# Soft-capped attention with a soft-MoE layer: head pairs on 128 partitions, column-tiled matmuls, slot sums inside the attention, casting weight loads

## Chip, cores, metric

One core of one Trainium2 chip. The metric is the device time of one execution in microseconds (us). Times are medians of all executions of a kernel. An execution more than 1.5% above the fastest of its kernel counts as slow, and the ratios leave it out.

The engines by their short names: PE multiplies matrices (its weight loads are counted apart), ACT applies functions such as tanh and exp, DVE does vector arithmetic and copies, POOL here casts v and issues the casting loads, and DMA moves data between memory and chip. PSUM is the memory that PE writes into. P·V is the product of the exps with v.

## The reference, cut to what matters

```python
# q, k, v: (8 batches, 12 heads, 448 positions, 64); q, k about 0.1 in size; cap = 30
scores = (1 / sqrt(64)) * q @ k.T
scores = cap * tanh(scores / cap)
x = softmax(scores) @ v                    # -> x: (3584, 768)
logits = x @ phi                           # phi: (768, 32), 8 experts x 4 slots
slot_input = softmax(logits, axis=0).T @ x # (32, 768): over all 3584 positions
slot_out[e] = relu(slot_input[e] @ w1[e]) @ w2[e]   # w1 (8,768,1024), w2 (8,1024,768)
out = softmax(logits, axis=1) @ slot_out   # (3584, 768)
```

All inputs are fp32: q, k and v are 33 MB, w1 and w2 25.2 MB each, the output 11 MB. No expert can start before the last position is through the attention.

## The kernel before

One head at a time. A head's 448 keys are four tiles of 112 partitions, so one tanh and one exp of 112x1792 elements cover it.

```python
for b in range(B):
    for h in range(H):
        # loads of q, k, v; cast of v; transposes of q and k in fp32; copies
        sc = psA.tile([C, NC, 512], F32, tag="sc")          # C = 112, NC = 4, one buffer
        for c in range(NC):
            nc.tensor.matmul(sc[:, c, :S], kT[:, c, :], qTf, start=True, stop=True)
        th = attn.tile([C, NC, S], BF16, tag="th")
        nc.scalar.activation(th, sc[:, :, :S], ACT.Tanh, scale=qk_scale / cap)
        ex = attn.tile([C, NC, S], BF16, tag="ex")
        nc.scalar.activation(ex, th, ACT.Exp, scale=cap)
        ot = psB.tile([Dh + 1, 512], F32, tag="ot", bufs=1)
        for c in range(NC):
            nc.tensor.matmul(ot[:, :S], vaug[:, c, :], ex[:, c, :],
                             start=(c == 0), stop=(c == NC - 1))
        # copy, transposes back, reciprocal, product -> xbuf
# after all heads: transposes of xbuf, logits, exp, transposes, slot sums   (cut)
for e in range(E):
    # w1 matmuls with 4 output rows, relu, transposes                       (cut)
    for fh in range(NFT // 2):
        w2f = moeW.tile([P, 2, D], F32, tag="w2f", bufs=3)
        nc.sync.dma_start(out=w2f, in_=w2r[:, e, 2 * fh:2 * fh + 2, :])
        nc.vector.tensor_copy(w2b[:, 2 * fh:2 * fh + 2, :], w2f)
    # w2 matmuls, transposes                                                (cut)
for nt in range(NNT):                                        # 32 stores
    # two matmuls into op
    osb = moeY.tile([C, 2, HD], F32, tag="osb")              # three buffers
    nc.scalar.mul(osb, op[:, :, :HD], Winv[:, nt:nt + 1])
    nc.sync.dma_start(out=dstap, in_=osb.rearrange("p a b -> p (a b)"))
```

The softmax here doesn't subtract the row's maximum and nothing guards it: scores larger than these inputs give would overflow.

## Time and profile before

| stage | from, to (us) | length | what fills it |
|---|---|---|---|
| start | 0 to 13.5 | 13.5 | loads, casts, transposes up to the first tanh |
| attention | 13.5 to 346 | 332 | ACT, tanh and exp |
| logits, slot sums | 346 to 394 | 48 | PE and ACT in turns, DMA nearly idle |
| experts | 394 to 472 | 78 | the load of w2 |
| output | 472 to 521 | 49 | stores from three buffers |

The stretches below are those stages in the trace of the kernel before. The columns are the stretch, its length, the busy time (and number of instructions) of PE, PE's weight loads, DVE, ACT and POOL, then PE's clock, the DMA share and GB/s.

```profile
13.00:346.00 333.00, 301.13 (x1901) 185.36 (x1900) 278.23 (x877) 313.09 (x192) 0.00 (x0) 0.97 0.54 167
346.00:394.00 48.00, 43.06 (x474) 25.63 (x473) 9.57 (x45) 31.91 (x102) 0.00 (x0) 0.73 0.22 81
394.00:472.00 78.00, 66.47 (x342) 24.95 (x340) 38.08 (x141) 16.22 (x32) 0.00 (x0) 0.80 0.80 275
472.00:521.00 49.00, 24.70 (x64) 11.74 (x63) 0.00 (x0) 28.59 (x32) 0.00 (x0) 0.50 0.71 225
```

ACT is busy for 313 of 333 us in the attention. In the 48 us after it the DMA share is 0.22, and up to 382 us it is 0.01 or less: nothing is loaded while the logits are made, and the experts then wait for w2.

### The profile page before, as it was taken

The numbers are of one execution on the slowest core, as the hardware profiler recorded it, in microseconds if no ns is written. First come the engines' busy times: TensorE is split into PE (matmuls) and PEld (weight loads), VectorE is DVE, ScalarE is ACT, GpSimd is POOL, SyncE is SP. The second block draws the span as 40 slices with busy tenths as digits, with TensorE's granted clock in tenths as the row PEclk, the third lists the DMA queues.
The fourth block names the chain that finished last, engine by engine and source line by source line (L and its number), as shares of the span: only waits on it lengthen the run. The fifth ranks groups of instructions, "written<-read, shape, count | busy, mean of one in ns | idle before, by whom it ended". The sixth has DMA issues, their size and how long they took to land.

```text
span 521.0 us, 8045 instructions
## 1 busy us (share of the span) xinstructions
PE 439.2 (84%) x2790; PEld 250.2 (48%) x2790; DVE 329.1 (63%) x1069; ACT 391.1 (75%) x359; POOL 1.3 (0%) x8
## 2 busy tenths in 40 slices
PE   2999898889999989999989998879979997766552
PEld 1555465555555555555555555534564333223220
DVE  2588678888888888888888889840044545441000
ACT  0689589999999999999999998966962231115664
POOL 0000000000000000000000000000000000000000
PEclk9999679999999999999999999965969999555555
DMA  8669555474565554565554533200059798964776
GB/s 242 229 183 316 163 160 170 132 248 126 180 187 186 178 180 133 171 187 187 173 182 134 180 108 97 66 8 0 1 193 355 255 328 284 316 208 153 245 244 205
DMA packets 57016, 95.00 MB, mean 182 GB/s; under 512 B 6800, under 2 KB 39056, under 8 KB 56976
## 3 DMA queue, kind: packets, MB, share of 16 engines
q1 hardware_dynamic: 56976, 94.49, 56.6%
q8 instruction: 22, 0.36, 0.3%
q14 instruction: 18, 0.15, 0.1%
HBM read 83.46 MB, written 11.01 MB: 181 GB/s over the span
## 4 chain that ended last, share of the span: by engine, by line
ACT 54%; PE 24%; DMA 14%; DVE 5%; issue 1%; SPq 1%; ACTq 0%; DVEq 0%
ACT ex L130 26%; ACT th L127 24%; DMA out_dram<-osb 6%; PE hp L234 4%; DMA w2f<-in_moe_w_dram 4%; PE sop L258 3%; PE xtp L182 3%; PE lt L190 3%; PE sc L123 3%; DMA vraw<-in_v_dram 2%; PE ot L134 2%; ACT osb L308 2%; PE qTp L108 2%; DVE w2b L253 1%; PE kTp L115 1%
## 5 line engine op out<-in xcount | busy, mean ns | idle before, releaser
L127 ACT ACTIVATE th<-sc 112x1792 bf16<-112x1792 f32 x96 | 158.1, 1647 | 27.0 <-PE sc L123 27.0
L130 ACT ACTIVATE ex<-th 112x1792 bf16<-112x1792 bf16 x96 | 162.9, 1697 | 3.0
L123 PE MATMUL sc<-qT,kT 64*112 64x448 bf16 x384 | 106.9, 372 | 17.7 <-ACT th L127 16.2
L134 PE MATMUL ot<-ex,vaug 112*65 112x448 bf16 x384 | 93.5, 367 | 9.2 <-ACT ex L130 8.8
L137 DVE CAST ot_sb<-ot 65x448 bf16<-65x448 f32 x96 | 59.5, 619 | 22.1 <-PE ot L134 20.2
L108 PE MATMUL qTp<-ident,qraw 112*64 112x112 f32 x384 | 62.6, 274 | 11.4 <-DVE qT L111 5.8
L148 DVE TENSOR_SCALAR xbuf<-ott,rec 112x64 bf16<-112x64 bf16 x384 | 68.3, 235 | 0.1
L123 PEld LDWEIGHTS <-kT 64*112 64x112 bf16 x384 | 44.7, 128 | 43.0 <-issue 31.0
L111 DVE CAST qT<-qTp 64x448 bf16<-64x448 f32 x96 | 58.3, 607 | 7.7 <-PE qTp L108 6.6
L115 PE MATMUL kTp<-ident,kraw 112*64 112x112 f32 x384 | 58.2, 272 | 0.8 <-DVE kT L118 0.7
L118 DVE CAST kT<-kTp 64x448 bf16<-64x448 f32 x96 | 57.1, 595 | 2.7 <-PE kTp L115 2.5
L134 PEld LDWEIGHTS <-vaug 112*65 112x65 bf16 x384 | 43.3, 114 | 31.2 <-issue 16.2
L108 PEld LDWEIGHTS qTp<-ident,qraw 112*64 112x64 f32 x384 | 36.6, 116 | 34.4 <-issue 11.4
L115 PEld LDWEIGHTS kTp<-ident,kraw 112*64 112x64 f32 x384 | 40.2, 117 | 13.5 <-issue 3.3
L141 PEld LDWEIGHTS <-ot_sb 65*112 65x112 bf16 x384 | 28.1, 134 | 37.6 <-DVE vaug L100 16.8
L308 ACT ACTIVATE osb<-op,Winv 112x768 f32<-112x768 f32 x32 | 28.6, 900 | 18.6 <-DMA out_dram<-osb 15.3
L141 PE MATMUL ott<-ident_bf,ot_sb 65*112 65x65 bf16 x384 | 38.6, 226 | 2.6 <-DVE ot_sb L137 2.6
L258 PE MATMUL sop<-w2b,hTb 128*4 128x384 bf16 x128 | 36.5, 393 | 4.2 <-DVE w2b L253 3.9
L303 PE MATMUL op<-so,ET 32*112 32x384 bf16 x64 | 24.8, 499 | 17.3 <-ACT osb L308 16.4
L253 DVE CAST w2b<-w2f 128x1536 bf16<-128x1536 f32 x32 | 30.3, 952 | 9.3 <-DMA w2f<-in_moe_w_dram 9.3
L263 ACT CAST sosb<-sop 4x384 bf16<-4x384 f32 x16 | 7.2, 467 | 36.8 <-PE sop L258 36.8
L146 DVE RECIPROCAL rec<-ott 112x4 f32<-112x4 bf16 x96 | 17.4, 181 | 23.4 <-PE ott L141 20.3
(44 smaller groups left out, 269.9 us busy)
## 6 DMA issues: line engine op xcount, KB each, us to landing
w1c<-in_moe_w_dram SPq DMA_DIRECT2D x24, 1024.0 KB, 5.5
w2f<-in_moe_w_dram SPq DMA_DIRECT2D x32, 768.0 KB, 5.9
qraw<-in_q_dram SPq DMA_DIRECT2D x96, 112.0 KB, 2.1
kraw<-in_k_dram SPq DMA_DIRECT2D x96, 112.0 KB, 2.1
vraw<-in_v_dram SPq DMA_DIRECT2D x96, 112.0 KB, 2.4
out_dram<-osb SPq DMA_DIRECT2D x32, 336.0 KB, 3.2
phic<-in_moe_phi_dram SPq DMA_DIRECT2D x1, 96.0 KB, 2.2
```

Source lines behind the costliest of these rows:

```text
L108: nc.tensor.transpose(qTp[:, c, :], qraw[:, c, :], ident[:C, :C])
L111: nc.vector.tensor_copy(qT, qTp)
L115: nc.tensor.transpose(kTp[:, c, :], kraw[:, c, :], ident[:C, :C])
L118: nc.vector.tensor_copy(kT, kTp)
L123: nc.tensor.matmul(sc[:, c, :S], kT[:, c, :], qTf, start=True, stop=True)
L127: nc.scalar.activation(th, sc[:, :, :S], ACT.Tanh, scale=qk_scale / cap)
L130: nc.scalar.activation(ex, th, ACT.Exp, scale=cap)
L134: nc.tensor.matmul(ot[:, :S], vaug[:, c, :], ex[:, c, :], start=(c == 0), stop=(c == NC - 1))
L137: nc.vector.tensor_copy(ot_sb, ot[:, :S])
L141: nc.tensor.transpose(ott[:, cq, :Dh + 1], ot_sb[:, cq * C:(cq + 1) * C], ident_bf[:Dh + 1, :Dh + 1])
L148: nc.vector.tensor_scalar_mul(xbuf[:, b * NC + cq, h * Dh:(h + 1) * Dh], ott[:, cq, :Dh], rec[:, cq:cq + 1])
L258: nc.tensor.matmul(sop[:, :HD], hTb[:, ft, :], w2b[:, ft, nch * HD:(nch + 1) * HD], start=(ft == 0), stop=(ft == NFT - 1))
```

## The change

The intent is to use all 128 partitions in the activations, to move the logits and slot sums into the attention, to load weights while the attention runs (cast on the way, so without DVE), and to let four experts share the PE array. Smaller parts go with it: q, k and v are loaded four heads at a time, and q and k are cast to bf16 before their transposes, which were in fp32.

A head pair has seven key tiles. A chunk is four tiles, counted through all pairs, so the end of a pair (its border) can fall inside a chunk.

```diff
-    C = 112                                  # one head, 4 key tiles of 112
+    CH = 4                                   # a chunk: 4 of the 7 x 48 key tiles
+    # a head pair (i = 0, 1) shares 128 partitions: 64 keys of each head
+    def qk_chunk(j):
+        sc = psS.tile([P, CH, 512], F32, name="sc", tag="sc")       # one buffer
+        for u in range(CH):
+            pr, c = divmod(j * CH + u, NT)
+            Q, h = divmod(pr, 2)
+            r = slice(h * HP, h * HP + HP)                  # row half by pair
+            for i in range(2):
+                cs = slice(i * HP, i * HP + HP)             # column half by head
+                pe.matmul(sc[cs, u, 0:S], qkT["k", Q][r, c, cs],
+                          qkT["q", Q][r, :, cs], start=True, stop=True)
 ...
+    def pv_tile(t):                          # V is block-diagonal: 128x130
+        if c == 0:
+            pvs[pr] = [psV.tile([P, 2, VW], F32, name=f"pv{s}", tag=f"pv{s}")
+                       for s in range(2)]                   # one buffer each
+        for g in range(NG):
+            pe.matmul(pvs[pr][g // 2][:, g % 2, :], exs[j][:, u, GOFF[g]:GOFF[g] + P],
+                      vbds[Q % 2][:, h, c, :], ...)
+        if c == NT - 1:                      # the pair's border
+            for s in range(2):
+                dve.reciprocal(rec, pv[:, :, :, DH:DH + 1])
+                dve.tensor_tensor(xq..., pv[:, :, :, 0:DH], rec..., op=ALU.mult)
 ...
+    for j in range(NCH):                     # 84 chunks
+        tanh_chunk(j)
+        if j > 0:
+            for t in range((j - 1) * CH, j * CH):
+                pv_tile(t)
+        for f, a in aux.pop(j, []):          # casts, transposes, logits, slot sums,
+            f(*a)                            # weight loads, spread over the chunks
+        if j + 1 < NCH:
+            qk_chunk(j + 1)
+        exp_chunk(j)
 ...
+        pool.dma_start(out=t, in_=w2_src(n0, 4))            # fp32 -> bf16 in the DMA
 ...
+                for gg in range(4):          # four experts on four column tiles
+                    pe.matmul(hp[32 * gg:32 * gg + NS, half, :], slT[:, jt, :],
+                              w1b[4 * i + gg][:, jt, half * 512:(half + 1) * 512], ...)
 ...
-        nc.scalar.mul(osb, op[:, :, :HD], Winv[:, nt:nt + 1])   # 3 buffers, ACT only
+        ob = wts.tile([P, 2, HD], F32, name="ob", tag="w1", bufs=E)   # 8 buffers
+        if n % 2:
+            dve.tensor_scalar_mul(ob, op[:, :, 0:HD], winv[:, n:n + 1])
+        else:
+            act.mul(ob, op[:, :, 0:HD], winv[:, n:n + 1])
```

## The prediction

> **What bounds the kernel now.** I read the page first, then the chain, then the groups, then the timeline of one steady stretch, then stretches of the span.
>
> ```profile
> span 521.0 us, 8045 instructions
> PE 439.2 (84%) x2790; PEld 250.2 (48%) x2790; DVE 329.1 (63%) x1069; ACT 391.1 (75%) x359; POOL 1.3 (0%) x8
> ...
> ACT  0689589999999999999999998966962231115664
> ...
> PEclk9999679999999999999999999965969999555555
> DMA  8669555474565554565554533200059798964776
> ```
>
> Three stages stand here. To slice 26 (about 345 us) ACT is full: attention. Then to slice 36 (470 us) ACT is nearly idle while DMA is high: logits, slot sums, experts. The last four are the output. The chain agrees: half of it is the two activations.
>
> ```profile
> ACT 54%; PE 24%; DMA 14%; DVE 5%; issue 1%; SPq 1%; ACTq 0%; DVEq 0%
> ...
> L127 ACT ACTIVATE th<-sc 112x1792 bf16<-112x1792 f32 x96 | 158.1, 1647 | 27.0 <-PE sc L123 27.0
> L130 ACT ACTIVATE ex<-th 112x1792 bf16<-112x1792 bf16 x96 | 162.9, 1697 | 3.0
> L308 ACT ACTIVATE osb<-op,Winv 112x768 f32<-112x768 f32 x32 | 28.6, 900 | 18.6 <-DMA out_dram<-osb 15.3
> ```
>
> Both activations use 112 of 128 partitions, and a head costs one of each. The timeline shows the steady step:
>
> ```profile
> 148.44 1.70 ACT L130 ACTIVATE ex<-th 112x1792 bf16<-112x1792 bf16 x1
> ...
> 150.04 1.65 ACT L127 ACTIVATE th<-sc 112x1792 bf16<-112x1792 f32 x1
> ...
> 150.19 0.92 PE L134 MATMUL ot<-ex,vaug 112*65 112x448 bf16 x4
> ...
> 151.72 1.70 ACT L130 ACTIVATE ex<-th 112x1792 bf16<-112x1792 bf16 x1
> ...
> 151.74 0.54 PE L123 MATMUL sc<-qT,kT 64*112 64x448 bf16 x2 [0.16 <-ACT th L127]
> ```
>
> From 148.44 to 151.72 is 3.28 us per head with no gap on ACT. The scores wait for the tanh before (there is one scores buffer), so PE has the 1.70 us of an exp to refill it. Four 448-column matmuls take 0.92 us: 187 ns each and about 0.17 us of latency.
>
> ```profile
> 150.00:345.00 195.00, 175.32 (x1160) 109.10 (x1159) 168.42 (x540) 191.82 (x119) 0.00 (x0) 0.99 0.48 149
> 400.00:410.00 10.00, 10.00 (x62) 3.75 (x60) 4.82 (x23) 3.32 (x7) 0.00 (x0) 1.00 0.86 291
> 490.00:500.00 10.00, 5.60 (x15) 2.67 (x15) 0.00 (x0) 6.30 (x7) 0.00 (x0) 0.50 0.77 241
> ```
>
> The columns are stretch, length, busy us of PE, PEld, DVE, ACT, POOL, then clock, DMA share, GB/s. The experts run at a DMA share of 0.86, so the fp32 w2 load (25.2 MB) sets their pace, about 340 GB/s at a full share. The output runs at 0.77 because only three output buffers rotate; a full share would be about 315 GB/s.
>
> **What the Trainium skill says.** (1) "TensorE: Matmul & The Clock Gate", Part 1 (HAM clock gate): PE runs at half rate until kept busy. The trace agrees: the same four matmuls took 0.92 us at 52.49 us and 1.70 us at 57.98 us, after some gaps.
>
> ```profile
> 52.49 0.92 PE L134 MATMUL ot<-ex,vaug 112*65 112x448 bf16 x4 [0.36 <-ACT ex L130]
> ...
> 57.98 1.70 PE L134 MATMUL ot<-ex,vaug 112*65 112x448 bf16 x4
> ```
>
> (2) Same page, Part 3 (row/col tiling): matmuls in different column tiles run together; three of 32 columns gave 2.38x. No run here shows it yet. (3) "DMA: Bandwidth & Descriptors", SWDGE vs HWDGE: a cast during DMA must be issued from GpSimd, whose software writes the descriptors. The kernel before has no such DMA. (4) "VectorE: DVE Perf Modes", perf-mode tier table: fp32 from PSUM runs at 1x, an fp32 SBUF copy at 2x. The trace agrees: 448 fp32 elements from PSUM took 619 ns, 1536 from SBUF 952 ns.
>
> **The change, part by part.** *Activations.* The 96 heads now fill 128 partitions: 48 pairs x 7 key tiles / 4 = 84 chunks of 128x1792, and length is set by the free size. 84 x 3.28 = 275.5 us against 96 x 3.28 = 315. Eight small exps of 128 elements (about 0.3 us, between the 185 ns and 530 ns rows) add 2.4: 278 us, against some 332 with today's gaps.
>
> *Start.* Today the first tanh waits until 13.5 us, behind a weight cast on DVE. Now: loads to 4 us, two casts, 14 transposes, two copies, eight cold matmuls: 10 us.
>
> *PE per chunk, warm.* P·V takes 16 matmuls of 130 columns; by 187 ns per 448 columns 54 ns each, say 58. Their 128-column weight loads hide: L219 did 192 matmuls with 128-column weights in 5.28 us, 27.5 ns each. That is 0.95 us. Transposes: 22 per 3.5 chunks at about 55 ns, 0.35 us. Logits and slot sums (N=32, 27 ns) 0.14. Scores: eight matmuls in pairs on two column tiles, 4 x 187 + 170 = 0.94 us if pairs overlap. Two tile-mode switches 0.25 (the gaps of 0.17 to 0.34 us before weight loads today). Sum 2.6 us, under 3.28.
>
> *A new wait.* The built program's order shows it: P·V of a new pair waits for DVE (two pv banks, one buffer each). A pair is 1.75 chunks, so in 36 of the 84 chunks the border falls inside the chunk. Then PE waits for reciprocal and product, twice: reciprocal 181 ns (L146); 256 PSUM elements, on the line through 4 (181) and 448 (619), 430 ns: 1.2 us, and 0.2 latency. In such a chunk P·V ends at about 2.45 us after the exp, transposes and logits add 0.38, switch 0.25, scores 1.0: 4.1 against 3.28. Stall 0.8 x 36 = 29 us.
>
> *Clock.* PE array work per chunk, some 2.1 us in 3.3 to 4.1, is thinner than today's (2.4 in 3.28), and today a single thin stretch cost 17 us at half clock. At half clock a chunk is about 5 us. I allow 14 us, some eight such chunks.
>
> *DVE and POOL* are no bound: per four heads DVE has two casts (0.64, on the line of 952 and 1201 ns), two PSUM copies (0.69), four pairs of normalisations (0.61), two x copies (0.5), 0.3: 6.4 us in 11.5.
>
> *Weights.* Half of w2 (12.6 MB) and all of w1 load during attention: 71 MB with q, k, v in 320 us, 220 GB/s, below 340. Of the other half, two of eight blocks' memory is free early; six (9.4 MB) overlie the last V and exp tiles and start after the last P·V: at 300 to 340 GB/s 28 to 31 us, and 2 for landing.
>
> *Tail beside it.* Last pair, logits, last slot sums 6; w1: 96 matmuls in column fours, at half clock 24 x 427 ns, 10; relu and transposes 2; eight E transposes with copies 7; sums 3; first half of w2 5: 33 us. Both sides are about level, so 36 us from the last exp to the slot outputs. This replaces today's 345 to 471 us, 126 us.
>
> *Output.* 28 stores of 393 KB with eight buffers, evacuated by ACT and DVE in turns (0.9 us each, 13 in all): 11.0 MB at 315 GB/s is 35 us, ends 3: 38, against 50.
>
> Sum: 10 + 278 + 29 + 14 + 36 + 38 = **405 us**.
>
> **Rivals.** *A, ACT stays bound*: the border waits fit in the slack, the clock stays warm. For it: PE sums to 2.6 us. Against: one scores buffer, and P·V ahead of the scores in PE's order. 10 + 278 + 5 + 33 + 36 = 362. *B, column tiles do not overlap*: scores take 8 x 187 + 170 = 1.67 us, the whole of an exp: borders stall 1.5 us, others 0.25, 66 in all; the expert matmuls add some 24: about 450. It would keep PE warmer. *C, casting DMAs are slow* (no trace shows one): at half rate the tail load is 55 us, about 430; worse if q, k, v starve behind it. *D, PE stays at half clock*: 84 x 5 = 420 for attention, over 500. Against: at half clock PE would be busy nearly always, which today brought the clock back within 17 us.
>
> **Range and chances.** Every stage loses work that the chain holds; the experts and slot sums alone give 90 us. Only D comes near the old time. A and B span most: 368 to 448. Faster 0.97, within 2% 0.015, slower 0.015.
>
> **What would show it.** Tanh and exp x84 at 1.65 and 1.70 us; scores at about 0.95 us per eight (pairs overlap) or 1.7 (B); tanh idle of about 43 us released by scores, and PE waits released by DVE's product in 36 chunks; POOL's w2 loads landing about 33 us after the last P·V; output at DMA share 0.9 or more. It is wrong if ACT's gaps are under 10 us (A), if scores take 1.7 us (B), if the tail waits much over 40 us for DMA (C), or if the clock row shows half rate through attention (D).

## The result and the profile after

The changed kernel takes 369.56 us (median of 4, 366.62 to 370.72) against 524.79 (median of 4, 521.68 to 529.73). The ratio is 0.7132, 95% interval 0.7046 to 0.7218. Ratios are the mean time of one kernel's fast runs over that of the fast runs of the kernel before, so they are not quite the ratio of the medians. The four runs of the kernel before that are given here would make it 0.703. The repeat below gives 0.7147.

First the head and rows of the page of the changed kernel, then its chain of waits by engine, and the costliest groups of the attention (line, engine, operation, output from input, shapes and count; busy us and mean ns; idle time before them and what ended it):

```profile
span 364.5 us, 7663 instructions
PE 256.4 (70%) x3316; PEld 171.0 (47%) x3316; DVE 158.5 (43%) x403; ACT 295.1 (81%) x198; POOL 79.5 (22%) x106
...
ACT  1798979999999999999999999999999980214341
...
PEclk9998969999999999999999999999999995969755
...
ACT 51%; PE 23%; DVE 11%; DMA 9%; issue 2%; SPq 0%; DVEq 0%; POOL 0%
...
L170 ACT ACTIVATE ex<-sc 128x1792 bf16<-128x1792 f32 x84 | 138.9, 1654 | 18.0 <-PE sc L164 17.9
L173 ACT ACTIVATE ex<-ex 128x1792 bf16<-128x1792 bf16 x84 | 142.5, 1696 | 2.4
...
L164 PE MATMUL sc<-qT,kT 64*64 64x448 bf16 x672 | 73.3, 369 | 4.6 <-ACT ex L170 1.9
```

The activations are 84 in place of 96, with unchanged lengths. Of the tanhs' 18 us of idle time, 8.9 are the start; 9.1 are all the gaps of the attention. The clock row is 9 almost throughout. The last two stages, in the columns of the table above:

```profile
299.70:332.20 32.50, 23.76 (x361) 14.47 (x362) 9.84 (x29) 4.11 (x8) 4.46 (x6) 0.74 0.83 146
332.20:364.50 32.30, 17.75 (x55) 6.09 (x54) 14.07 (x14) 12.51 (x14) 0.00 (x0) 0.64 0.88 341
```

The last exp ends at 299.70 us and the slot outputs stand at 332.2. So the attention ends 46 us earlier than before; 126 us between it and the output have become 32.5; and the output takes 32.3 instead of 49.

Last, one chunk with a pair border, on its three engines (start, length, then the wait before it in brackets):

```profile
151.50 1.70 ACT L173 ACTIVATE ex<-ex 128x1792 bf16<-128x1792 bf16 x1
...
153.25 0.40 PE L185 MATMUL pv<-vbd,ex 128*128 128x130 bf16 x4 [0.79 <-ACT ex L173]
153.58 0.18 DVE L194 RECIPROCAL rec<-pv 128x4 f32<-128x4 f32 x1 [1.41 <-PE pv L185]
153.79 0.42 DVE L195 TENSOR_TENSOR xq<-pv,rec 128x256 bf16<-128x256 f32 x1
...
154.28 0.29 PE L185 MATMUL pv<-vbd,ex 128*128 128x130 bf16 x2 [0.62 <-DVE xq L195]
...
154.83 0.74 PE L185 MATMUL pv<-vbd,ex 128*128 128x130 bf16 x10 [0.26 <-DVE xq L195]
...
155.41 0.36 PE L217 MATMUL lps<-phib,xT 128*128 128x32 bf16 x8
...
155.69 0.94 PE L164 MATMUL sc<-qT,kT 64*64 64x448 bf16 x8
...
156.68 1.66 ACT L170 ACTIVATE ex<-sc 128x1792 bf16<-128x1792 f32 x1 [0.20 <-PE sc L164]
```

The exp ends at 153.20. PE does one key tile of the old pair, waits 0.62 and 0.26 us for DVE's two products, finishes P·V, does the logits, then the scores. They end at 156.63, 3.43 us after the exp. Tanh was free at 156.48 and lost 0.20 us.

### The profile page after: what moved, and what is told of

Read it like the earlier page. It is cut to its first block, busy times and chain, and to the rows that moved or that the text cites. A ratio compares the mean times of both kernels' runs of the same rounds, so it can differ in the third digit from the quotient of the medians.

```text
span 364.5 us, 7663 instructions
## 1 busy us (share of the span) xinstructions
PE 256.4 (70%) x3316; PEld 171.0 (47%) x3316; DVE 158.5 (43%) x403; ACT 295.1 (81%) x198; POOL 79.5 (22%) x106
## 4 chain that ended last, share of the span: by engine, by line
ACT 51%; PE 23%; DVE 11%; DMA 9%; issue 2%; SPq 0%; DVEq 0%; POOL 0%
ACT ex L173 26%; ACT ex L170 25%; PE pv L185 9%; PE sc L164 7%; DVE xq L195 5%; DMA w2t<-in_moe_w_dram 5%; DMA out_dram<-ob 3%; DVE ob L405 2%; PE so_ps L388 2%; DVE rec L194 2%; PE kps L134 2%; DMA kraw<-in_k_dram 1%; PE op L401 1%; PE qps L134 1%; DVE qT L136 1%
## 5 line engine op out<-in xcount | busy, mean ns | idle before, releaser
L185 PE MATMUL pv<-vbd,ex 128*128 128x130 bf16 x1344 | 107.0, 225 | 69.0 <-ACT ex L173 36.5
L170 ACT ACTIVATE ex<-sc 128x1792 bf16<-128x1792 f32 x84 | 138.9, 1654 | 18.0 <-PE sc L164 17.9
L173 ACT ACTIVATE ex<-ex 128x1792 bf16<-128x1792 bf16 x84 | 142.5, 1696 | 2.4
L185 PEld LDWEIGHTS <-ex 128*128 128x128 bf16 x1344 | 79.8, 100 | 116.1 <-ACT ex L173 71.2
L164 PE MATMUL sc<-qT,kT 64*64 64x448 bf16 x672 | 73.3, 369 | 4.6 <-ACT ex L170 1.9
L144 POOL CAST vbd<-vraw 64x896 bf16<-64x896 f32 x24 | 22.3, 928 | 203.2 <-PE pv L185 199.6
L195 DVE TENSOR_TENSOR xq<-pv,rec 128x256 bf16<-128x256 f32 x96 | 40.8, 425 | 3.3
L164 PEld LDWEIGHTS <-kT 64*64 64x64 bf16 x672 | 29.1, 107 | 20.3 <-issue 3.3
L209 DVE COPY xT<-xps 128x512 bf16<-128x512 bf16 x48 | 20.1, 418 | 14.2 <-PE xps L207 14.2
L145 POOL CAST vbd<-vraw 64x896 bf16<-64x896 f32 x24 | 23.0, 957 | 1.4
L207 PE MATMUL xps<-ident,xq 128*128 128x128 bf16 x192 | 19.3, 223 | 3.9 <-DVE qT L136 3.7
L136 DVE COPY kT<-kps 128x896 bf16<-128x896 bf16 x24 | 14.9, 620 | 12.7 <-PE kps L134 12.7
```

The lines of the kernel that those rows point to most:

```text
L136: dve.tensor_copy(t, ps)
L144: pool.tensor_copy(t[0:HP, :, :, 0:DH], raw[0:HP])
L145: pool.tensor_copy(t[HP:P, :, :, DH + 1:VW - 1], raw[HP:P])
L164: pe.matmul(sc[cs, u, 0:S], qkT["k", Q][r, c, cs], qkT["q", Q][r, :, cs], start=True, stop=True)
L170: act.activation(ex, scores.pop(j)[:, :, 0:S], ACT.Tanh, scale=qk_scale / cap)
L173: act.activation(exs[j], exs[j], ACT.Exp, scale=cap)
```

## The experiments

Eleven kernels were run, each against the kernel before. The first is the changed kernel again, as the yardstick: a difference of ratios times some 520 us gives us. The intervals of the ratios are 2 to 5 us wide on either side, so a difference of under some 4 us is read from traces or not at all.

**The changed kernel again.** No edit.

> The changed kernel once more, unaltered, as the yardstick for the runs beside it. All theories: 366 to 371 us, ratio to the kernel before 0.70 to 0.72, tanh idle of about 18 us of which 9 are the start.

370.57 us, ratio 0.7147 (0.7091 to 0.7203), as expected but for the attention: its gaps were 12.7 us, with six over 0.6 us where the first trace had two. So the gaps of one execution vary by some 4 us.

**Same-column matmuls issued next to each other.**

```diff
-        for u in range(CH):
-            for i in range(2):
+        for i in range(2):
+            for u in range(CH):
```

> Same score matmuls, reordered: first the four of the left column half, then the four of the right, so that no two neighbours lie on different column tiles. Theory (pairs overlap, and PE has almost no slack in chunks with a pair border): eight take 1.67 us instead of 0.94; gaps before tanh of about 1.0 us in 36 chunks and 0.15 in the others, 43 us in place of 9, so about 403 us. Rival B of the prediction (column tiles do not overlap anyway): no change, 369.

371.53 us, ratio 0.7179 (0.7121 to 0.7236): no change, and the expected 403 was missed. That looks like rival B, but the trace says otherwise:

```profile
152.30 0.95 PE L164 MATMUL sc<-qT,kT 64*64 64x448 bf16 x8
```

Four on the left column half and then four on the right still take 0.95 us together. So either the halves work at the same time whatever the order of issue, or overlap has nothing to do with columns. This run could not tell the two apart; the next was made to.

**Both matmuls over all 128 columns.**

```diff
-                pe.matmul(sc[cs, u, 0:S], qkT["k", Q][r, c, cs],
+                pe.matmul(sc[:, u, 0:S], qkT["k", Q][r, c, :],
```

This computes something else: the second matmul overwrites the first, so half of the keys meet the other head's queries. (With q and k of size 0.1 the weights are close to uniform, and the comparison with the reference passed all the same.)

> Each of the two score matmuls of a key tile is spread over all 128 columns instead of one half, so that no two can lie side by side (the result is wrong on purpose). Theory (the pairs of column tiles do overlap, whatever the order in which they are issued): eight take 1.67 us instead of 0.94, gaps of about 1.0 us in 36 chunks and 0.15 in the others, 43 us in place of some 9 to 13, so about 400 us as long as the clock stays up. Rival (the 0.94 us has nothing to do with column halves, for instance because 64 rows go through faster): no change, 370.

402.42 us, ratio 0.7812 (0.7755 to 0.787): 32 to 35 us more, as the theory said. Scores of two chunks, and the tanh after the first:

```profile
151.81 1.68 PE L164 MATMUL sc<-qT,kT 64*128 64x448 bf16 x8
...
153.53 1.66 ACT L170 ACTIVATE ex<-sc 128x1792 bf16<-128x1792 f32 x1 [1.00 <-PE sc L164]
...
156.07 0.94 PE L164 MATMUL sc<-qT,kT 64*128 64x448 bf16 x8
```

Without column halves eight take 1.68 us. The second chunk takes 0.94 because it holds two key tiles of one pair and two of the next, which lie on different row halves. I sorted the score groups of all chunks by how many key tiles lie on one row half and on the other, and took the most frequent length:

| tiles per row half | chunks | after the change | all columns |
|---|---|---|---|
| 4 and 0 | 48 | 0.94 us | 1.67 |
| 3 and 1 (or 1 and 3) | 24 | 0.76 | 1.29 to 1.31 |
| 2 and 2 | 12 | 0.58 | 0.94 |

One rule gives them all: every row half with every column half works through its own matmuls, at 187 ns each, beside the others; the group takes the longest of these lines plus some 0.2 us. (4 x 187, 3 x 187, 2 x 187 ns on the left; 8, 6 and 4 on the right.) Five of the 48 groups of the last run took 3.16 us, at half rate, so a part of its 32 to 35 us is the clock's.

**The new pair's P·V after the scores.**

```diff
-            for t in range((j - 1) * CH, j * CH):
-                pv_tile(t)
+            ts = list(range((j - 1) * CH, j * CH))
+            nb = next((n for n in range(1, CH) if ts[n] % NT == 0), CH)
+            for t in ts[:nb]:                # the old pair
+                pv_tile(t)
         # aux, then qk_chunk(j + 1)
+        if j > 0:
+            for t in ts[nb:]:                # the new pair
+                pv_tile(t)
```

> In a chunk with a pair border, P.V of the new pair is issued after the scores of the next chunk, so that the scores no longer stand behind PE's wait for the normalisation; nothing else moves. Theory (the 9 us of gaps before tanh come from that wait): gaps in attention fall to under 2 us, and the time by 6 to 9 us, to 361 to 363. Rival (the gaps come from transposes, late q/k loads or the clock): under 2 us gained. Second rival (the new pair's P.V now delays the next chunk): gaps move, no gain.

363.28 us, ratio 0.7028 (0.6985 to 0.7071): 6 to 7 us gained, as expected. The gaps of 0.2 to 0.4 us at the borders are gone (8 gaps under 0.6 us, 2.4 us in all, against 23 with 6.2 us in the yardstick). But 9.1 us of gaps are left, not under 2: four are of 0.9 to 2.0 us, one of them at the start. The other three are where PE's clock fell. Here is the stretch ahead of one, and its scores:

```profile
65.00:68.40 3.40, 2.04 (x36) 1.50 (x36) 1.92 (x6) 3.37 (x3) 0.00 (x0) 1.00 0.28 46
...
75.20:78.60 3.40, 1.80 (x26) 1.11 (x24) 2.04 (x7) 3.37 (x3) 0.00 (x0) 0.97 1.03 218
```
```profile
78.67 1.70 PE L164 MATMUL sc<-qT,kT 64*64 64x448 bf16 x8 [0.96 <-ACT ex L170]
```

PE was busy for 1.80 of 3.40 us, then ran at half rate: eight scores in 1.70 us instead of 0.94. At 65 us, with 2.04 busy, the clock stayed up. The theory missed this part: waiting for tanh instead of DVE keeps the path short but leaves PE as idle.

These two stretches give no threshold of busy time. The clock records of this trace change only on a grid of 3.41 us. In the grid windows ahead of the three falls PE was busy for 1.99, 2.08 and 2.39 us; three windows with 1.96 were followed by no fall. Another measure sorts them: each matmul's columns at 448 per 187 ns, times the share of the 128x128 array that it uses. This comes to 1.04, 1.07 and 1.15 us ahead of the three falls, and to 1.29 us or more in the 72 other full-rate windows of this attention. It is a sorting after the fact that no run tests, and its figure does not carry over: the kernel before kept its clock through windows of less than 0.9 us.

**The product done twice at each border.** The same `tensor_tensor` is issued a second time.

> The normalising product on DVE is done twice at each pair border (the same result written again), 2 x 0.43 us more in the wait of PE for DVE. Theory (border chunks have used up their slack, so each further us of border counts): 36 mid-chunk borders x some 0.75 to 0.85 us, 27 to 31 us more, about 397. Rival A of the prediction (border waits lie in slack): under 5 us more.

442.67 us, ratio 0.8529 (0.8426 to 0.8632): 72 us more, over twice what the wait alone should cost. The page shows where the rest is from:

```profile
PE 327.3 (74%) x3316; PEld 220.5 (50%) x3316; DVE 199.2 (45%) x499; ACT 298.8 (68%) x198; POOL 79.4 (18%) x106
...
PEclk9966866866867668668667668885886676586965
```

The same 3316 matmuls keep PE busy for 327 us instead of 262.5 in the yardstick. PE's clock is down in a large part of the attention. The reading: a longer wait at the border makes PE thin, the clock falls, and the next chunk is late too. The next two runs test it.

**The reciprocal done twice.** A smaller dose of the same, 2 x 0.18 us per border.

> The reciprocal at each border is done twice: 2 x 0.18 us more in the wait, where doing the product twice added 2 x 0.46. Theory (what made the doubled product cost 72 us instead of 31 is PE's clock, which falls when a border leaves PE idle too long): wait alone, 36 x 0.36 = 13 us; if the clock falls here too, much more than 13, some 25 to 35, with PE busy rising for the same instructions. Rival (each us of border costs in proportion, 72 us for 0.92): 28 us with PE busy unchanged. If it is 13 or less with PE busy unchanged, the fall comes only beyond this length.

412.21 us, ratio 0.7943 (0.7894 to 0.7993): 41 us more, above even the expected 25 to 35. Its page:

```profile
PE 306.1 (75%) x3316; PEld 205.5 (50%) x3316; DVE 176.0 (43%) x499; ACT 297.8 (73%) x198; POOL 79.4 (19%) x106
...
PEclk9997998767768669987677887888876797588855
```

0.36 us in 36 borders is 13 us; the clock makes 41 of it, with PE busy 44 us longer for the same work. PE's waits for DVE's reciprocal and product grew by only 15 us (from 32.0 to 47.1). There is hardly a margin: the changed kernel lies near the point from which its clock falls often.

**Product twice, with the new pair's P·V after the scores.** The two edits together.

> The doubled product again (72 us slower by itself), now with the new pair's P.V after the scores. Theory (DVE's extra work costs only where the scores stand behind PE's wait for it, and the clock falls because of that wait): nearly all of the 72 us goes away, at most 5 us over the 363 of the reordered kernel, with PE busy near 255 us. Rival (the extra DVE work costs by itself, by delaying the transposes' copies or by idling PE so that its clock falls in any order): 385 us or more, with PE busy well over 270.

369.51 us, ratio 0.7111 (0.7049 to 0.7173): 4 to 6 us over the reordered kernel, where the same DVE work cost 72 us before. PE is busy 272.6 us, more than the 255 expected (the rival had "well over 270"), so some chunks still run at half clock. But most of the cost was not DVE's work as such: it was where the scores stood, behind PE's wait for it.

**No load of w2 in the tail.** The second half's loads are left out and the first half is used twice (a wrong result).

```diff
-        return w2b[:, n, :] if n < R2 else w2t[(n - R2) // 4][:, (n - R2) % 4, :]
+        return w2b[:, n % R2, :]
```

> The loads of the second half of w2 are left out and the first half is used twice (wrong on purpose), so nothing of the tail can wait for a DMA. Theory (the stretch from the last exp to the slot outputs is a chain on PE, DVE and ACT): no more than 2 us gained, under 0.6%. Rival of the prediction (loading takes 30 to 33 us and sets this stretch, or is level with it): 3 us or more gained, and much more by its rival C.

368.24 us, ratio 0.7158 (0.7118 to 0.7198): no change. The w2 matmuls, first with the loads (the kernel after the change), then without:

```profile
323.85 4.59 PE L388 MATMUL so_ps<-w2b,hpad 128*32 128x384 bf16 x64
...
328.27 2.77 PE L388 MATMUL so_ps<-w2t,hpad 128*32 128x384 bf16 x64
```
```profile
324.52 7.54 PE L382 MATMUL so_ps<-w2b,hpad 128*32 128x384 bf16 x128
```

With the loads there is no wait before the second half either, and the tail takes 32.3 us without them against 32.5. So it is a chain of small steps on PE, DVE and ACT. (The chain by engine puts 17 us of the tail, from 303.74 us, down to a load of w2t. Leaving the loads out shows that this releaser was wrongly inferred.)

**All of w2 after the attention.** The first half's loads leave the chunk loop and are issued ahead of the second half's.

> The first half of w2 is no longer loaded between the attention chunks but issued after them on the same queue, where POOL reaches it at about 279 us, ahead of the second half. Theory (the tail hides only one half of w2): 25.2 MB of fp32 from 279 us at some 350 GB/s (38.6% of 16 engines' 364.5 us for 50.3 MB read) end at about 353 us, instead of slot outputs at 332: 20 to 24 us slower, about 391. Rival (the tail hides all of it, or DMA runs faster when alone): under 5 us slower.

384.65 us, ratio 0.7475 (0.7419 to 0.7532): 17 us more, somewhat less than the 20 to 24 expected. The tail hides one half of w2, but not all of it.

**Three output buffers.**

```diff
-        ob = wts.tile([P, 2, HD], F32, name="ob", tag="w1", bufs=E)
+        ob = obs[n % 3]                      # three tiles made before the loop
```

> Three output buffers in turns instead of eight, as in the kernel before; two engines still empty PSUM. Theory (the number of stores in flight set the old rate): a buffer is taken for 0.9 to 1.0 us of evacuation and 3.2 us to landing, three stores in some 4.2 us, 28 in 39 us, instead of 31: 8 us slower, about 378, DMA share 0.77 or less in the output. Rival (one engine that emptied PSUM set the old rate, and two are enough): under 2 us slower.

376.23 us, ratio 0.7313 (0.7271 to 0.7355): 6 to 9 us more. Ten us in the middle of the output, with eight buffers and with three:

```profile
344.00:354.00 10.00, 8.57 (x22) 2.66 (x21) 5.09 (x5) 5.06 (x6) 0.00 (x0) 0.50 1.02 399
```
```profile
346.00:356.00 10.00, 6.70 (x18) 2.02 (x16) 4.43 (x5) 3.60 (x4) 0.00 (x0) 0.50 0.87 343
```

The buffers in flight, not the second engine, give 399 instead of 343 GB/s. But three buffers do not bring the old output back: it takes 39.0 us here (333.1 to 372.1), 32.3 with eight and 49 in the kernel before, and the share was 0.87, not 0.77 or less. So the number of buffers makes some 7 of the 17 us. The other 10 came with the rest of the change (a second engine, 28 stores of 384 KB instead of 32 of 336 KB), which no run takes apart.

**A version that beats both.** The new pair's P·V after the scores, and a rearranged tail: `hpad` is cleared by POOL, and the transposes of E (the exps of the logits) lie between the w1 matmuls of the second expert group (the first group's own transposes come earlier too).

```diff
-    dve.memset(hpad, 0.0)
+    pool.memset(hpad, 0.0)
 ...
                               start=(jt == 0), stop=(jt == NJ - 1))
+                if i == 1 and jt in (0, 2, 4, 5):
+                    e_transp(4 * half + (0, 2, 4, 5).index(jt))
```

> Two changes together: the new pair's P.V after the scores (measured alone at 7 us), and a rearranged tail: hpad cleared by POOL instead of DVE ahead of the slot inputs (0.91 us), the eight transposes of E and their copies laid between the matmuls of the second expert group (today 5.7 us by themselves, of which PE needs some 2), which should also keep PE's clock up for the first half of the slot outputs (4.6 us at half clock against 2.8). Theory (the tail is a chain on the engines and not on the DMA): 5 to 6 us less in the tail, 12 to 13 us in all, about 357. Rival (w2's second half then sets the end: 9.4 MB of fp32 after the last P.V, seen moving at 210 GB/s of written bytes, 22 to 24 us and 4 of issue, so at 328 at the earliest): only 3 us in the tail, about 360.

361.09 us (358.44 to 362.54), ratio 0.6966 (0.6931 to 0.7001): the fastest of all, 9.5 us under the yardstick. The tail gave only 3 us more, as the rival said:

```profile
318.41 2.45 PE L403 MATMUL so_ps<-w2t,hpad 128*32 128x384 bf16 x56
322.49 0.51 PE L403 MATMUL so_ps<-w2t,hpad 128*32 128x384 bf16 x8 [1.63 <-DMA w2t<-in_moe_w_dram]
```

Now the last eight matmuls do wait, for the last load. In the changed kernel that load landed at 328.1 us and was used at 330.4: the chain had stood only some 2 us above the DMA.

## Why the prediction was right or wrong

The time lay in the range, but only just (369.56 in 368 to 448), 35 us under the point. One term, border stall and clock, is 34 us too large; the other errors are small and partly cancel. The profiled execution, term by term:

| term | predicted | measured |
|---|---|---|
| start to the first tanh | 10 | 10.9 |
| ACT's work, first tanh to last exp without gaps | 278 | 279.7 |
| border stall and clock | 29 + 14 | 9.1 |
| last exp to slot outputs | 36 | 32.5 |
| output | 38 | 32.3 |
| sum | 405 | 364.5 |

The timed median is 5 us above this span: this execution was the fastest of the four, and its own time was 366.6.

**Start and ACT's work** were right: the same lengths, 84 of each.

**"Stall 0.8 x 36 = 29 us" is the step that failed.** The wait of PE for DVE is there, in the form foretold. But the sum 2.45 + 0.38 + 0.25 + 1.0 = 4.1 us for a border chunk was too long. (Its own terms for P·V, 0.95 + 1.2 + 0.2, make 2.35; where the 2.45 is from is not said.) The chunk shown took 2.21 to the start of the logits, 0.28 to the start of the scores, and 0.94 for them: 3.43. The switch of tile mode (from 128x128 matmuls to 64x64 ones), 0.25, did not appear: scores started before the logits' modelled end. And the last 0.08 to 0.16 us of each part overlaps the next one (the logits start 0.16 before the modelled end of P·V); I had counted it in each.

Second, the scores do not always take 1.0. Two chunks after a border the scores can span two pairs, which lie on different row halves. So they took 0.58 where the border fell after three tiles, 0.76 after two and 0.94 after one. Sorting the first trace's gaps by kind of chunk: 0.4 us in the 12 borders of the first kind, 4.7 in the 12 of the second (2.3 of them in two gaps of 0.8 us or more), 2.6 in the 11 followed by a tanh of the third, and 1.4 elsewhere. That is 7.7 us at borders instead of 29.

**"Eight such chunks at half clock", 14 us**, was not met either. The repeat has six gaps over 0.6 us, 6.6 us in all, and the first trace two, 2.3 us; not all of them are the clock's. But the fear was sound: 0.36 us more at each border brought it on and cost 41 us. The clock stays up here by less than that per border chunk, so keeping the 14 us was in part luck.

**The tail** was close: 32.5 against 36, in part by luck. The steps of the side-chain estimate of 33, up to the first half of w2, took 28.6 (299.7 to 328.3): the w1 matmuls and relus 8.4 instead of 10 and more, with the clock up for part of them (48 in 2.77 us, four side by side; one after another, at 187 ns per 448 columns, they would need 10). The second half and the copies, which it left out, took 4.0. The DMA side ended some 2 us sooner than needed, 26.9 us after the last P·V. Between 308 and 326 us the loads moved 210 GB/s of bf16, that is 420 GB/s of fp32 read, and I had taken 300 to 340.

**Output**: more stores in flight did raise the rate, but by the run with three buffers they explain 7 of the 17 us; the size was off too. I had put a full share at 315 GB/s, from 241 at a share of 0.77; the stores ran at 399 GB/s and a share of 1.02.

**The rivals.** A (362 us) came nearest. By the prediction's own sign, gaps under 10 us, the first trace (9.1) speaks for A and the repeat (12.7) against it. Its premise of slack fell with the doubled reciprocal and product. B fell: the column halves overlap. Its size was nearly right: without the overlap the kernel is 32 to 35 us slower, where B put 66 us of stalls in place of 29. C fell: the casting loads read 420 GB/s of fp32 in the tail, where the plain loads of the experts before moved 291. D is what the doubled product runs into in part.

## What to carry to other kernels

When one engine is full and another waits for a third just ahead of feeding it, put the work that feeds the full engine before that wait; here it took no resource, and it turned a cost of 72 us for extra DVE work into 4 to 6. Before adding a few tenths of a us to PE's waits, look at how near its clock is to falling: what counts is the half-rate chunk that follows, not the wait. And build the length of a chunk from the starts of its instructions, since adding lengths counts each pipeline latency again.

## What the Trainium skill lacked or had wrong

- "TensorE: Matmul & The Clock Gate", Part 3 (what overlaps and what doesn't), says that matmuls start and end strictly in the order of issue. With four on the left column half issued ahead of four on the right, the eight took 0.95 us. In strict order the fifth could start only with or after the fourth, at 3 x 187 ns, and the eighth 3 x 187 ns later still, so they would have ended after 1.4 us or more. (This takes PE to get them in the kernel's order, which no view shows.) Matmuls on the same columns and rows did not overlap (1.68 us for eight).
- The same page, Part 1 (HAM clock gate), names an idle window of about 3.4 us, and warns of idle gaps longer than that; it also tells of a kernel whose clock swung through short idles, without saying how short or how many. Here the clock fell with no PE wait over 1.0 us in the stretch. How thin a window counts as idle is on no page, and busy time alone does not tell it: 1.99, 2.08 and 2.39 of 3.41 us were followed by falls, 1.96 by none.
- No page gives a rate for loads that cast on the way: 210 GB/s of bf16 written, 420 GB/s of fp32 read, with no other transfer beside them (308 to 326 us).
